# A three-stage network on one core: a first operation without data for ScalarE, other loads, and a new order of every engine's work

## The chip, the cores and the metric

The kernel runs on one core of a Trainium2 chip. Five engines work side by side: TensorE multiplies matrices (PE in the profile, and PEld for its weight loads), VectorE (DVE), ScalarE (ACT) and GpSimd (POOL) do elementwise work, and SyncE (SP) issues the DMAs that move data between HBM and the on-chip memory SBUF. TensorE writes into PSUM, which has eight banks. The metric is the device time of one execution in microseconds (us).

## The reference

Three networks stand behind each other, all in float32, for 2 batches of 768 positions.

1. Attention with 8 heads of 64 columns. A query sees the keys less than 16 positions away, and beside them 24 summaries of all keys: the maximum of each block of 32 keys, with the mean of the 32 values:

```python
k_sum = k.reshape(B, H, nb, block, D).max(axis=3)
v_sum = v.reshape(B, H, nb, block, D).mean(axis=3)
mask_l = np.abs(pos[:, None] - pos[None, :]) < window      # window = 16, block = 32
scores_l = np.where(mask_l, scale * q @ k.T, -1e9)
scores_s = scale * q @ k_sum.T + np.log(block)
a = softmax(concat([scores_l, scores_s]))
x = a @ concat([v, v_sum])
```

2. Four causal attention experts (`wq, wk, wv, wo`, 64 columns each) over the result, of which a gate (`w_gate`) mixes the best two for each position.
3. A channel mix: `k = max(xk @ w_k, 0)`, `out = sigmoid(xr @ w_r) * ((k * k) @ w_v)`, where `xk` and `xr` blend each position with the one before it.

## The kernel before

**Tiles.** Stage 1 works through 12 tiles of 128 queries, six to a batch. For each: scores (`stage1_scores`; the mask is added and the row's maximum taken by VectorE at L606, which leaves the maximum in `nm`), the exponential on ScalarE (L609, 8 a tile), the sum and its reciprocal (`rss`, L612 and L614), the normalizing product (L620 on GpSimd or VectorE, L625 on ScalarE), transposes on TensorE (`turn`, L637), and the product with the values (L679). The values' block means are matmuls too (L500), which need the values of a whole batch. Stage 2 has projections (L772 for values and gates, L754 for queries and keys), scores (L854), transposes (L637), weighted values (L952) and the output projection (L994). Stage 3 has L1146 (`rec`), L1197 (`hid`) and L1284 (`duo`); its two large products use seven block products in place of eight.

**Precision.** Operands of stages 2 and 3 are split into a high and a low half (`rnd`, L368 to L371, and `sub`, L376 to L378), and each product is three matmuls: high by high, high by low, low by high.

**Shapes of TensorE's array.** Stages 2 and 3 mostly use the whole array (128 by 128). The scores of both attentions, the transposes and the products with values use parts of it at once: 64 by 64 (L583, L588, L589), 64 rows by 128 (L637, L854), 128 rows by 64 columns (L679, L952), 128 rows by 24 (L500). Below these are called shapes, and work that follows other work of the same shape is one run.

**Loads.** All are issued by SP in one queue (`load`, L359), with at most eight at a time in flight: the ninth waits for the first. First come the queries of tile 0 and the keys of batch 0, one load for each of the four head pairs (`key_sums`), into one tile `ks` with zeros at both ends (the halo); VectorE takes their block maxima (`ksm`, L486). A slab is a tile's own piece of the keys, copied from `ks` for batch 0 and loaded for batch 1 (`slab`). The value tiles `v` (`load_v`) hold 96 rows of values and 24 rows of means, the latter written by some engine once the means are there (`put_val_sums`).

**The order.** Nothing is reordered at run time. Each step is recorded as an operation, and the table `ORDER` gives the sequence in which they are issued, four numbers to an operation, of which the remainder picks the engine where several can do it (`any_of`). `HOMES` gives each tile its buffer. An engine works through its part of the sequence strictly in turn and waits where an operand is not ready.

Of the kernel before, what the change touches and what calls it, by code (L numbers as in the profile page):

```python
# [10 lines left out]
AF = mybir.ActivationFunctionType  # L11
# [303 lines left out]
def attn_moe_rwkv(  # L315
    ctx: ExitStack,
    tc: tile.TileContext,
    qT: bass.AP,
    kS: bass.AP,
    vp: bass.AP,  # L320
    wqk: bass.AP,
    wvg: bass.AP,
# [1165 lines left out]
```

## Time and profile before

| | us |
|---|---|
| three runs | 334.40, 332.78, 333.82 (median 333.82) |
| the profiled execution | 332.78 |
| its span, first to last instruction | 331.0 |
| TensorE busy | 319.1 |
| VectorE busy | 311.3 |
| ScalarE busy | 266.8 |
| GpSimd busy | 114.0 |

The profiled execution is the fastest of the three and lies 1.04 us below their median; 1.8 us of it lie outside the span. TensorE's granted clock is 1.0 in every stretch. Busy times say how much an engine did, not who waits for whom: for that the waits of TensorE and the chain of work that ended last are read.

### The profile page before, as it was taken

The numbers are of one execution on the slowest core, as the hardware profiler recorded it, in microseconds if no ns is written. First come the engines' busy times: TensorE is split into PE (matmuls) and PEld (weight loads), VectorE is DVE, ScalarE is ACT, GpSimd is POOL, SyncE is SP. The second block draws the span as 40 slices with busy tenths as digits, with TensorE's granted clock in tenths as the row PEclk, the third lists the DMA queues.
The fourth block names the chain that finished last, engine by engine and source line by source line (L and its number), as shares of the span: only waits on it lengthen the run. The fifth ranks groups of instructions, "written<-read, shape, count | busy, mean of one in ns | idle before, by whom it ended". The sixth has DMA issues, their size and how long they took to land.

```text
span 331.0 us, 8978 instructions
## 1 busy us (share of the span) xinstructions
PE 319.1 (96%) x3296; PEld 286.8 (87%) x3296; DVE 311.3 (94%) x941; ACT 266.8 (81%) x777; POOL 114.0 (34%) x127
## 2 busy tenths in 40 slices
PE   3979999999999999999999999999999999999995
PEld 2869988888789879787776899999998899999995
DVE  3789999999999899989999999999999999999996
ACT  0989999999898779779887889889799988965360
POOL 0556872768303810432310001545036000360231
PEclk9999999999999999999999999999999999999999
DMA  7996985757242000111212001100050000021033
GB/s 247 400 395 204 305 301 189 270 152 248 92 137 64 4 0 10 59 63 65 87 43 63 3 4 61 63 0 3 0 183 10 0 0 2 18 79 52 0 113 128
DMA packets 19628, 34.08 MB, mean 103 GB/s; under 512 B 2080, under 2 KB 8480, under 8 KB 19584
## 3 DMA queue, kind: packets, MB, share of 16 engines
q1 hardware_dynamic: 19584, 33.51, 30.0%
q8 instruction: 26, 0.43, 0.5%
q14 instruction: 18, 0.15, 0.1%
HBM read 30.16 MB, written 3.15 MB: 101 GB/s over the span
## 4 chain that ended last, share of the span: by engine, by line
PE 94%; DVE 2%; DMA 2%; SPq 1%; issue 0%; ACT 0%; ACTq 0%
PE ps L1284 18%; PE ps L1197 18%; PE ps L754 11%; PE ps L1146 10%; PE ps L637 6%; PE ps L952 6%; PE ps L772 6%; PE ps L854 6%; PE ps L994 5%; PE ps L679 3%; PE ps L583 3%; DMA ks<-in_kS 2%; PE ps L588 1%; PE ps L500 1%; DVE w L606 1%; SPq L359 1%
## 5 line engine op out<-in xcount | busy, mean ns | idle before, releaser
L1284 PE MATMUL ps<-w,s 128*128 128x256 f32 x336 | 48.7, 281 | 0.0
L1284 PEld LDWEIGHTS ps<-w,s 128*128 128x128 f32 x336 | 43.9, 188 | 0.1
L1197 PE MATMUL ps<-b,w 128*128 128x384 f32 x216 | 40.3, 337 | 0.0
L1197 PEld LDWEIGHTS ps<-b,w 128*128 128x128 f32 x216 | 38.0, 188 | 0.1
L368 ACT ACTIVATE t<-ps 128x192 f32<-128x192 f32 (+1 forms) x108 | 30.9, 356 | 8.6 <-PE ps L637 4.2
L754 PE MATMUL ps<-b,w 128*128 128x384 f32 x192 | 36.6, 341 | 0.0
L1146 PE MATMUL ps<-w,b 128*128 128x512 f32 x144 | 35.8, 398 | 0.0
L754 PEld LDWEIGHTS ps<-b,w 128*128 128x128 f32 x192 | 33.2, 188 | 0.9 <-issue 0.4
L1146 PEld LDWEIGHTS ps<-w,b 128*128 128x128 f32 x144 | 26.5, 188 | 5.9 <-DVE gsum L820 0.2
L609 ACT ACTIVATE w<-w,nm 128x120 f32<-128x120 f32 x72 | 28.5, 407 | 0.9 <-DVE nm L606 0.7
L368 ACT ACTIVATE b<-ps 128x384 f32<-128x384 f32 (+4 forms) x50 | 23.8, 492 | 3.9 <-PE ps L994 1.6
L368 ACT ACTIVATE s<-u 128x512 fp32r<-128x512 f32 x24 | 14.8, 628 | 9.4 <-DVE u L1059 5.5
L1123 DVE SCALAR_TENSOR_TENSOR t<-b,mu,t 128x384 f32<-128x384 f32 x32 | 21.2, 681 | 0.8 <-ACT t L387 0.7
L854 PE MATMUL ps<-ks,b 64*128 64x384 f32 (+3 forms) x192 | 21.8, 342 | 0.0
L368 ACT ACTIVATE w<-ps 120x256 f32<-120x256 f32 (+2 forms) x49 | 19.7, 445 | 1.7 <-PE ps L1146 0.8
L952 PE MATMUL ps<-t,b 128*64 128x384 f32 (+2 forms) x144 | 20.7, 422 | 0.0
L376 DVE TENSOR_TENSOR b<-t,b 128x384 fp32r<-128x384 f32 x37 | 20.1, 567 | 0.5 <-ACT b L368 0.3
L772 PE MATMUL ps<-q,b 128*128 128x260 f32 x144 | 20.3, 290 | 0.2 <-DVE b L376 0.2
L772 PEld LDWEIGHTS ps<-q,b 128*128 128x128 f32 x144 | 18.2, 188 | 1.6 <-issue 0.5
L368 ACT ACTIVATE b<-t 128x384 fp32r<-128x384 f32 x38 | 19.0, 516 | 0.5 <-PE ps L1197 0.5
L994 PE MATMUL ps<-u,w 128*128 128x384 f32 x96 | 18.9, 338 | 0.0
L387 ACT ACTIVATE t<-b,omu 128x384 f32<-128x384 f32 x28 | 16.9, 613 | 2.2 <-PE ps L952 1.6
(202 smaller groups left out, 913.4 us busy)
## 6 DMA issues: line engine op xcount, KB each, us to landing
s<-in_wk SPq DMA_DIRECT2D x8, 512.0 KB, 4.0
s<-in_wv SPq DMA_DIRECT2D x8, 512.0 KB, 4.2
w<-in_vp SPq DMA_DIRECT2D x15, 256.0 KB, 6.5
w<-in_qT SPq DMA_DIRECT2D x12, 256.0 KB, 5.6
out_y<-t SPq DMA_DIRECT2D x24, 128.0 KB, 1.8
s<-in_wr SPq DMA_DIRECT2D x4, 512.0 KB, 5.7
s<-in_kS SPq DMA_DIRECT2D x6, 320.0 KB, 4.7
ks<-in_kS SPq DMA_DIRECT2D x4, 400.0 KB, 3.9
```

Of the source, the lines that this page charges most:

```text
L368: ways = [("act", act(n, sb), lambda: nc.scalar.activation(dst(), src(), AF.Copy)), ("dve", dve2(n) if sb else dve(n), lambda: nc.vector.t ...
L376: ways = [("dve", dve(n), lambda: nc.vector.tensor_tensor(dst(), a(), b().bitcast(F32), ALU.subtract), sb)]
L609: op("act", act(NK, True) + 186, lambda i=i, z=z, pr=pr, nm=nm: nc.scalar.activation(pr()[:, i], pr()[:, i], AF.Exp, bias=nm.t[:, i:i + 1] ...
L754: mm(p.t[:, :C], a[kc].t[:, cols], x.t[:, kc, :], start=(kc == 0 and i == 0), stop=(kc == KC - 1 and i == 2))
L772: mm(p.t[:, :260], x.t[:, kc, tok], a[kc].t, start=(kc == 0 and i == 0), stop=(kc == KC - 1 and i == 2))
L854: mm(ps[e2].t[:, :z - a], q1.t[r, x, tok], ks.t[r, y, a:z], start=n == 0, stop=n == 2)
L952: mm(acc.t[64 * e2:64 * e2 + 64, tq0 * P:(tq0 + cnt) * P], vv.t[:, kb, e * D:(e + 1) * D], th[e2].t[:, i0 * P:(i0 + cnt) * P], start=first ...
L994: mm(p.t[:, :C], a[ep].t[:, m * P:(m + 1) * P], x.t[:, ep, :], start=(ep == 0 and i == 0), stop=(ep == 1 and i == 2))
L1123: op("dve", dve(C) + 60, lambda: nc.vector.scalar_tensor_tensor(tmp(), cur(), mu.t[:, i:i + 1], tmp(), ALU.mult, ALU.add), r=rd, w=[(mb, m ...
L1146: mm(p.t, a.t[:, kc, tok], w[2](), start=(kc == 0 and i == 0), stop=(kc == KC - 1 and i == 2))
L1197: mm(p.t[:, :C], a[2]()[:, o:o + P], x.t[:, u, j], start=not (j or i), stop=j == 1 and i == 2)
L1284: mm(p.t[:, :256], x.t[:, u, j * P:(j + 1) * P], v[2]()[:, col:col + 256], start=not (j or i), stop=j == FC // 2 - 1 and i == 2)
```

## The change

- ScalarE gets a first operation that needs no data: an exponential of a small constant tile, written to `omu`, which a later operation overwrites.
- The keys stand in HBM a second time: contiguous for each head pair (`kA`) and, for batch 1, for each tile with its halo (`kT`). Batch 0's key loads carry 768 columns in place of 800; GpSimd writes the halo's zeros.
- Value tiles other than the first load their 96 own rows, where before those of the first eight tiles loaded 128.
- The three masks are three loads, the third later; the identity in `cst` is 64 columns wide in place of 128.
- `ORDER` and `HOMES` are new throughout: the order of every engine, the engine of some steps and the buffers.

```diff
@@ buffers and first operations
-    cst = buf("cst", [P, P + OWN + 16 + 2 * PAIR])
+    cst = buf("cst", [P, SUB + OWN + 16 + 2 * PAIR])
...
+    op("act", 210, lambda: nc.scalar.activation(omu.t[:, 0:1], sms.t[:, 0, 0, 1:2], AF.Exp), r=[(sms, "eps")], w=[omu])
@@ def slab(t):
-            load(lambda: k.t[:, :, NB:NB + SLAB], kS[b, :, :, tt * P:tt * P + SLAB], P * HP * SLAB * 4, 290.0,
+            load(lambda: k.t[:, :, NB:NB + SLAB], kT[tt], P * HP * SLAB * 4, 340.0,
@@ def load_v(t, s2):
-        if t < TPB + 2:
+        if t < PLAIN:
             load(lambda: v.t, vp[b, a:a + P], P * 2048, w=[(v, "win"), (v, "sum")])
         else:
             a = SUB * (2 * tt + s2) + NB
-            load(lambda: v.t[WROW[s2]], vp[b, a:a + KS0], KS0 * 2048, 230.0, w=[(v, "win")])
+            load(lambda: v.t[WROW[s2]], vp[b, a:a + KS0], KS0 * 2048, 330.0, w=[(v, "win")])
@@ def turn(banks_, c, src):
-            nc.tensor.transpose(banks_[a].t[:v.shape[1], c * SUB:(c + 1) * SUB], v, cst.t[r, r])
+            nc.tensor.transpose(banks_[a].t[:v.shape[1], c * SUB:(c + 1) * SUB], v, cst.t[r, :SUB])
@@ def raw64(src, n=1):  (the number is the planner's, not the operation's)
-        op("act", act(512, True) + 60, lambda: nc.scalar.activation(ff(), high(), AF.Abs, scale=F64_SCALE),
+        op("act", 660, lambda: nc.scalar.activation(ff(), high(), AF.Abs, scale=F64_SCALE),
@@ first loads
+    op("pool", 150, lambda: (nc.gpsimd.memset(k0.t[:, :, :HALO], 0.0), nc.gpsimd.memset(k0.t[:, :, HALO + S:], 0.0)),
+       w=[(k0, "halo")])
     load_q(0)
     for i in range(HP):
-        key_sums(0, i, k0, (lambda i=i: k0.t[:, i], lambda i=i: k0.t[:, i, HALO:HALO + S]), kS[0, :, i])
+        key_sums(0, i, k0, [lambda i=i: k0.t[:, i, HALO:HALO + S]] * 2, kA[0, i])
...
-    load(lambda: msk.t[:, 1:], masks[:, 1:], P * 2 * NK * 4, 260.0, w=[(msk, 1)])
-    load(lambda: cst.t, consts, P * 1120, 300.0, w=[cst])
+    load(lambda: msk.t[:, 1], masks[:, 1], P * NK * 4, 260.0, w=[(msk, 1)])
+    load(lambda: cst.t, consts, P * 864, 300.0, w=[cst])
@@ the order, one line of each
-    12, 0, 4, 16, 36, 44, 24, 32, 56, 52, 64, 20, 60, 236, 72, 40, 92, 48, 244, 201, 68, 28, 188, 280, 100, 792,
...
+    8032, 8172, 8036, 8052, 8008, 8176, 8012, 8141, 8224, 8180, 8192, 8056, 8144, 8228, 8060, 8232, 8064, 8196,
```

Lines after the change are one or two off: L583 is L582, L606 is L605, L637 is L636, L772 is L771, L500 is L502.

Three places show how the order moves. The first is the head of SP's queue: `w` takes queries or values, `ks` keys, `msk` masks, `b_57` the weights of values and gates (`in_wvg`). Before:

```order
L359 DMA w_63<-in_qT 128x512
L359 DMA ks_69<-in_kS 128x800 x4
L359 DMA msk_74<-in_masks 128x120
L359 DMA msk_74<-in_masks 128x240
L359 DMA w_77<-in_qT 128x512
L359 DMA w_79<-in_qT 128x512
L359 DMA cst_83<-in_consts 128x280
```

The same place after the change:

```order
L360 DMA w_63<-in_qT 128x512
L360 DMA ks_67<-in_kA 128x768 x4
L360 DMA msk_78<-in_masks 128x120
L360 DMA w_80<-in_qT 128x512
L360 DMA b_57_82<-in_wvg 128x1040
L360 DMA msk_78<-in_masks 128x120
L360 DMA w_87<-in_qT 128x512
L360 DMA cst_90<-in_consts 128x216
```

The weights of values and gates, 20th among the rows before, are now fifth, behind the keys. Further down, four loads of means from the tile `w_416` into value tiles (L541) have come into this queue, at rows 25, 27, 29 and 31, writes that GpSimd and ScalarE made before; ScalarE makes none now (before five).

The second place is VectorE in the softmax of tile 0 (`b_60`, maxima in `nm`), as it passes to tile 1 (`b_72`). Before:

```order
L606 ISA b_60_87,nm_89<-ps_135,msk_74 128x120
L606 ISA nm_89 128x1
L606 ISA b_60_87,nm_88<-ps_104,msk_74 128x120
L606 ISA nm_88 128x1
L606 ISA b_72_156,nm_158<-ps_155,msk_74 128x120
```

After the change, where `q_199`, `q_204` and `q_209` are halves of the weights `b_57`, and `s_16` is a slab that takes key maxima:

```order
L605 ISA b_60_94,nm_95<-ps_116,msk_78 128x120
L605 ISA nm_95 128x1
L370 CAST q_204<-b_57_82 128x260
L377 TENSOR_TENSOR q_209<-b_57_82,q_199 128x260
L370 COPY s_16_153<-ksm_85 128x4x24
L605 ISA b_60_94,nm_95<-ps_92,msk_78 128x120
L605 ISA nm_95 128x1
L605 ISA b_72_158,nm_159<-ps_156,msk_78 128x120
```

Three operations have come between the seventh and the eighth maximum of tile 0. `q_199` is made by GpSimd.

The third place is TensorE late in stage 2, where turns (L637, then L636) of the tile `t` stand before a product with the values (L952, then L951). Before:

```order
L1146 MATMUL ps_3425<-w_1181,b_676_3065 128x512
L637 MATMUL ps_3436<-cst_83,t_3423 128x64
L637 MATMUL ps_3437<-cst_83,t_3423 128x64
...
L952 MATMUL ps_3444<-t_3375,b_403_2105 64x384
L952 MATMUL ps_3444<-t_3390,b_403_2105 64x384
```

After the change (six turns of the tile in both lists, two of them shown):

```order
L636 MATMUL ps_3431<-cst_90,u_638_3261 128x64
L636 MATMUL ps_3448<-cst_90,t_3421 128x64
L636 MATMUL ps_3449<-cst_90,t_3421 128x64
...
L951 MATMUL ps_3457<-t_3359,b_403_2135 64x384
L951 MATMUL ps_3457<-t_3380,b_403_2135 64x384
```

The turns of `t` now follow other turns, where before they followed a product on the whole array. Over the whole list the number of runs by shape is this, where the first L772 is the first matmul of stage 2:

| runs of one shape | whole array | 64 rows by 128 | 128 by 64 | 64 by 64 | 128 by 24 | sum |
|---|---|---|---|---|---|---|
| before, up to the first L772 | 0 | 3 | 2 | 4 | 3 | 12 |
| after, up to the first L771 | 0 | 4 | 2 | 3 | 4 | 13 |
| before, from there on | 23 | 33 | 16 | 6 | 2 | 80 |
| after, from there on | 18 | 27 | 16 | 6 | 2 | 69 |

The matmuls themselves are the same in number on every line, on either side of that point.

## Rows read from the trace of the kernel before

**Rows 1.** The page, busy time of each engine: us, share of the span, instructions.

```profile
PE 319.1 (96%) x3296; PEld 286.8 (87%) x3296; DVE 311.3 (94%) x941; ACT 266.8 (81%) x777; POOL 114.0 (34%) x127
```

**Rows 2.** Waits of TensorE: who waited for whom, total us, times, longest.

```profile
PE ps L588 <- DMA ks<-in_kS: 4.7, 1, 4.7
PE ps L583 <- ACT b L625: 1.7, 1, 1.7
PE ps L589 <- DVE ksm L486: 1.4, 4, 0.4
PE ps L772 <- DVE b L376: 0.2, 1, 0.2
```

**Rows 3.** Busy time by stretch: length, then PE, PEld, DVE, ACT, POOL; clock, DMA share.

```profile
0.00:26.50 26.50, 18.37 (x456) 15.28 (x456) 17.50 (x96) 16.19 (x63) 10.89 (x23) 1.00 0.95 345
26.50:60.00 33.50, 33.49 (x477) 30.45 (x481) 32.51 (x133) 31.94 (x137) 21.35 (x24) 1.00 0.75 254
270.00:327.20 57.20, 57.20 (x482) 56.92 (x481) 56.60 (x118) 35.51 (x71) 15.45 (x8) 1.00 0.15 50
327.20:331.00 3.80, 0.01 (x1) 0.00 (x0) 0.85 (x2) 0.00 (x0) 0.00 (x0) 1.00 0.30 104
```

**Rows 4.** The same view, VectorE alone, seven stretches from 26.5 to 327.2.

```profile
sum 300.70, DVE 292.95; mean DVE 41.85
```

**Rows 5.** The chain that ended last, early: start, us, what.

```profile
2.60 6.08 DMA ks<-in_kS
...
24.33 0.42 DVE q L369 x2
24.74 0.91 DVE q L376
...
26.51 1.53 PE ps L772 x9
```

**Rows 6.** The chain later, on TensorE.

```profile
76.95 0.72 PE ps L854 x6
77.68 0.18 PE ps L637 x6
...
98.66 1.58 PE ps L994 x9
100.24 2.10 PE ps L754 x12
...
104.44 2.11 PE ps L994 x12
106.55 0.33 PE ps L637 x6
106.88 2.30 PE ps L754 x12
```

**Rows 7.** Timeline of ScalarE, early: start, us, operation.

```profile
8.77 1.28 ACT L368 ACT_TABLE_LOAD   x1 [8.77 <-DMA ks<-in_kS]
...
10.88 0.38 ACT L609 ACTIVATE b<-b,nm 128x120 f32<-128x120 f32 x1
```

**Rows 8.** Timeline of VectorE: the first maximum read, and a copy at 40.7.

```profile
9.77 0.08 DVE L606 DVE_READ_ACCUMULATOR2_ANT nm<- 128x1 f32 x1
...
40.74 0.96 DVE L369 COPY s<-ksm 128x96 f32<-128x96 f32 x1
```

**Rows 9.** Timeline of GpSimd: weights rounded at 29.5, a product at 40.7.

```profile
29.51 1.06 POOL L371 TENSOR_SCALAR w<-s 128x512 fp32r<-128x512 f32 x1
...
40.65 0.99 POOL L620 TENSOR_TENSOR w<-w,rss 128x480 f32<-128x480 f32 x1
```

**Rows 10.** The page, DMA issues: KB each, median us from issue to landing.

```profile
s<-in_wqk SPq DMA_DIRECT2D x2, 512.0 KB, 6.6
```

**Rows 11.** Groups by line and shape: the low half of an operand, GpSimd and VectorE.

```profile
L378 POOL TENSOR_TENSOR s<-u,s 128x512 fp32r<-128x512 f32 x1 | 3.0, 3046 | 5.3 <-ACT s L368 5.3
L376 DVE TENSOR_TENSOR s<-u,s 128x512 fp32r<-128x512 f32 x23 | 16.2, 711 | 0.0
```

More of the change, by code (lines that the diff above doesn't have):

```diff
@@ L318, in attn_moe_rwkv @@
     qT: bass.AP,
-    kS: bass.AP,
+    kA: bass.AP,
+    kT: bass.AP,
     vp: bass.AP,
@@ L466, in slab @@
             rnd("dve", lambda: k.t[:, :, NB:NB + SLAB], lambda: k0.t[:, :, tt * P:tt * P + SLAB], HP * SLAB,
-                [(k0, i) for i in range(HP)], [(k, "win")], True)
+                [k0], [(k, "win")], True)
     def load_v(t, s2):
@@ L484, in key_sums @@
             ksm[b] = buf("ksm", [P, HP, NB])
-        load(tf[0], src, P * (S if b else SPV) * 4, w=[(tb, i)])
+        load(tf[0], src, P * S * 4, w=[(tb, i)])
         op("dve", dve(S), lambda: nc.vector.tensor_reduce(
@@ L521, in sums1 @@
             t = buf("s4", [P, S])
-            key_sums(1, i, t, [lambda t=t: t.t] * 2, kS[1, :, i, HALO:HALO + S])
+            key_sums(1, i, t, [lambda t=t: t.t] * 2, kA[1, i])
         p = [bank("ps")] * 2
@@ L540, in put_val_sums @@
             ], r=[vsm[b]], w=[(v, "sum")], issue=850)
-    def ident():
-        return cst.t[:, 0:P]
     def own(j, s2=None):
-        o = P + OWN - NB - 4 * j
+        o = SUB + OWN - NB - 4 * j
         if s2 is not None:
-            o = P + OWN + 16 + s2 * PAIR + NB - 2 - (4 * j + 2 * s2)
+            o = SUB + OWN + 16 + s2 * PAIR + NB - 2 - (4 * j + 2 * s2)
         return cst.t[:, o:o + NB]
@@ L570, in stage1_scores @@
             ps = [bank("ps") for par in range(2)]
-            kr = [(x, i) for x in (k0, ksm[0]) for i in range(lo, hi)] if t < EARLY else [k]
+            kr = [(x, i) for x in (k0, ksm[0]) for i in range(lo, hi)] + [(k0, "halo")] if t < EARLY else [k]
             for i in range(lo, hi):
@@ L607, in stage1_softmax @@
                     pr()[:, i], p.t[:, i * NK:(i + 1) * NK], msk.t[:, m], -0.125, BIG, ALU.add, ALU.min,
-                    nm.t[:, i:i + 1]), r=[(p, i), (msk, min(m, 1))], w=[key[i], (nm, i)])
+                    nm.t[:, i:i + 1]), r=[(p, i), (msk, m)], w=[key[i], (nm, i)])
                 op("act", act(NK, True) + 186, lambda i=i, z=z, pr=pr, nm=nm: nc.scalar.activation(
@@ L798, in lt @@
         def lt():
-            return cst.t[:, P + OWN:P + OWN + 16].rearrange("p (o a c) -> p o a c", o=1, a=E).to_broadcast(sh)
+            return cst.t[:, SUB + OWN:SUB + OWN + 16].rearrange("p (o a c) -> p o a c", o=1, a=E).to_broadcast(sh)
         def wide(v):
@@ L1346, in attn_moe_rwkv @@
     load_q(3)
+    load(lambda: msk.t[:, 2], masks[:, 2], P * NK * 4, 260.0, w=[(msk, 2)])
     load(lambda: mu.t, mus, 4096, w=[mu])
@@ L1414, in attn_moe_rwkv @@
     plan.run(alloc)
-_ORDER = ["qT", "kS", "vp", "wqk", "wvg", "wo", "wk", "wv", "wr", "mus", "masks", "tri", "consts"]
+_ORDER = ["qT", "kA", "kT", "vp", "wqk", "wvg", "wo", "wk", "wv", "wr", "mus", "masks", "tri", "consts"]
 def _layout(
@@ L1427, in _layout @@
     ks[..., HALO:HALO + S] = k.reshape(B, HP, 2, S, D).transpose(0, 2, 4, 1, 3)
-    d["kS"] = ks.reshape(B, P, HP, SPV)
+    d["kA"] = k.reshape(B, HP, 2, S, D).transpose(0, 1, 2, 4, 3).reshape(B, HP, P, S)
+    ks = ks[1].reshape(P, HP, SPV)
+    d["kT"] = np.stack([ks[:, :, t * P:t * P + SLAB] for t in range(TPB)])
     vp = np.zeros((B, VROWS, DM), f)
@@ L1466, in _layout @@
     lt = np.broadcast_to((np.arange(E)[None, :] < np.arange(E)[:, None]).astype(f).reshape(1, 16), (P, 16))
-    d["consts"] = np.concatenate([np.eye(P, dtype=f), own, lt, pair.reshape(P, 2 * PAIR)], axis=1)
+    d["consts"] = np.concatenate([np.tile(np.eye(SUB, dtype=f), (2, 1)), own, lt, pair.reshape(P, 2 * PAIR)], axis=1)
     return d
```

276 rows, old and new, of tables (HOMES, ORDER) are left out of this document.

## The prediction

> **What bounds the kernel now.** I read the busy times first: TensorE works 319.1 of 331.0 us and VectorE 311.3 [rows 1], so either could be the bound. The waits decide: TensorE waits 4.7 us for the first keys, 1.4 for key maxima, 1.7 at a score, 0.2 at its first projection, and at nothing else worth a row [rows 2]. By stretch, it is idle 8.1 us before 26.5 us (26.50 less 18.37), hardly at all from there to 327.2, and 3.8 us at the end, when the last result is added, multiplied and stored [rows 3]. VectorE is nearly as full: 292.95 of those 300.7 us [rows 4]. The kernel thus has three parts: a start up to the first projection at 26.51 us [rows 5], 300.7 us in which matmuls stand end to end, and a tail. With equal matmuls, time can come from an earlier start, from what TensorE loses between matmuls, and from the tail.
>
> One such loss shows in the chain. Twelve matmuls of L754 take 2.10 us behind L994, which uses the whole array too, and 2.30 behind turns: 0.20 for going back to the whole array. Six turns take 0.18 us behind L854, of the same shape, and 0.33 behind L994: 0.15 for entering a divided shape [rows 6]. A busy TensorE hides these, since the profile counts them as work.
>
> **The change part by part.**
>
> *Fewer changes of shape.* From the first projection on there are 80 runs of one shape before and 69 after. Runs on the whole array fall from 23 to 18: 5 times 0.20 is 1.0 us. The others fall from 57 to 51: 6 times 0.15 is 0.9. Together 1.9 us, in the stretch where TensorE is never idle, so the whole of it counts, if its operands come as much sooner. VectorE must follow: by the changed counts in the two orders, each times its group's mean duration, its 311.3 us fall by about 3.8 (the largest piece is three `s<-u,s` fewer at 0.71, 2.1 us [rows 11]; additional copies take some of it back), while ScalarE gains about 1.1 us and GpSimd about 3.6, with 64 and 217 us idle [rows 1]. So VectorE doesn't become the bound by its sum. With 11 runs at 0.15 to 0.20 each, the term lies between 1.65 and 2.2.
>
> *ScalarE's first operation.* The table load, 1.28 us, began at 8.77 when the last keys had landed, then a slab copy, and the first exponential stood at 10.88 [rows 7], though its maximum was read by 9.85 (9.77 and 0.08) [rows 8]. With the load in idle time before the keys, the exponentials can start some 0.9 us sooner; the slab copy stays ahead of them. At worst nothing, if another engine is last.
>
> *Keys and their halo.* The four key loads are 1,536 KB in place of 1,600. The last landed 6.08 us after its issue began [rows 5], with the others in front: 64 of 1,600 of that is 0.24 us; I take 0.2. Contiguity I cost at nothing; no row has such a load alone. GpSimd writes the zeros in its first two microseconds, while the keys are on their way. `kT` and the smaller constants come where no DMA is waited for [rows 2]; the third mask is needed only by tile 5. Nothing for these.
>
> *Value rows.* Fourteen loads lose 64 KB each, 0.9 MB. In the first 26.5 us the DMA engines are 95% busy, at 345 GB/s [rows 3], so the four or five of them that lie there save at most about 0.9 us of transfers. TensorE waits there for no values: 0, at best 0.9.
>
> *Weights of values and gates.* Moved from 20th to fifth in SP's queue, behind the keys and the second queries, 520 KB earlier than some masks, queries, constants and values. These have time: TensorE takes up the first values only after the scores of three tiles. In return VectorE's casts and low halves of these weights, 0.42 and 0.91 us on the chain at 24.33 [rows 5], come away from the spot just ahead of the first projection: up to 1.3 us. But two of them, and a copy of key maxima, now stand ahead of the eighth maximum of tile 0, and ScalarE's exponential of it, with all of tile 1's behind, waits for that.
>
> What this costs hangs on GpSimd. The trace has such a copy at 40.74: it took 0.96 us for 96 elements a partition, and ended as a GpSimd product begun at 40.65 ended, 0.99 later [rows 8, 9]. It was held up. In the new place GpSimd is rounding the same weights. If each of the three is held up for most of a GpSimd operation, some 0.5 us each, ScalarE loses about 1.5 us; if none, nothing. The Trainium skill, in SBUF — State Buffer, section "Who interferes with whom", says that a VectorE copy or cast in its faster mode, or an operation on two SBUF inputs beside a GpSimd read, shares a port pair with GpSimd that is held for the whole instruction, so that the later one waits. The trace agrees at 40.74.
>
> *Means through SP.* Four small loads now wait in SP's queue for the means. Behind them stand the second half of the weights of queries and keys, batch 1's keys, the triangle mask, the output weights. In the old kernel GpSimd took up that half at 29.51 [rows 9]. Such loads take 6.6 us to land [rows 10], so one issued by 22.9 is in time. I expect the means near 20; cost 0, and up to 2 us if they came 2 us after 22.9. ScalarE is rid of five writes, before the first projection and soon after.
>
> *Start, summed.* 0.2 for the keys, up to 0.9 for ScalarE, up to 1.3 for the weights: 2.4 at best; 0 when the copies are held up. I take the middle, 1.2. One more run of a shape in the start costs 0.15 at most and is in that. The tail has the same steps in the same order: 0.
>
> *Sum.* 1.9 and 1.2 make 3.1 us. The profiled execution, 332.78, becomes 329.7; it lies 1.04 below the median of 333.82, so a median of **330.7 us** is my forecast. Its own range is 329.0 to 332.0.
>
> **The rivals.**
>
> *The three copies are held up.* If GpSimd blocks each, as at 40.74 [rows 8, 9], the 1.5 us on ScalarE's chain outweigh its 0.9 and most of the weights' gain; the start comes out even and only the runs pay: 332.78 less 1.9 and plus 1.04, 331.9. For it speaks the one case that the trace has; against it, that the weights may land when GpSimd is between two operations. This is what the rule of SBUF — State Buffer would make of the new place.
>
> *The time comes back as waits.* The early gain goes as above, and inside the long stretch VectorE, at 97% [rows 4], is late now and then by a tenth or two, since a new order over so many steps has new tight spots; ten or so of those eat the 1.9. For it: VectorE's share, and that a search aims at planned times, not real ones. Against it: the old order was such a plan too, and TensorE waits 0.2 us in its long stretch. The time would be 333 to 334, say 333.5.
>
> *Slower: low halves on GpSimd in the last stage.* Four operands of L1284 get their low half `s<-u,s` from GpSimd, where before it was one, and two others of a like kind. GpSimd takes 3.05 us for it, VectorE 0.71 [rows 11]. Where the product stands less than 3 us behind its high half, TensorE waits up to 2.3 us each, 9.4 in all, in a stretch with no slack. That gives 330.7 and 9.4, 340.1 at most. It decides against the change once more than 4.8 us of it show: three of the four uncovered. Against it: the one before was covered, and GpSimd idles for most of that stretch, 15.45 of 57.2 us busy [rows 3].
>
> *Everything early pays.* The start gains 2.4, the runs 2.2 and the lighter DMA load 0.5: 5.1 off, 328.7.
>
> **How the numbers follow.** Chances: forecast 0.50, copies held up 0.20, waits 0.16, slower 0.08, everything early 0.06. About 0.5% (1.7 us) is what a measurement of this kernel can tell from no change. Faster by more than that is below 332.15: nearly all of the forecast's share, over half of the first rival's and the last case, 0.66. Within 0.5% is the rest of these and the waits, 0.25. Slower is 0.09: the GpSimd case and a little of the waits. For 8 times in 10 the range reaches from the last case, 328.7, to the second rival's 333.6.
>
> **What would show it.** In the new profile the table load should end before 4 us and the first exponential start near 10.0. The first L771 should start near 25.3 (26.51 less 1.2), with L605 of tile 0's eighth maximum after 12 us if the copies are held up. From there to the last matmul should be 298.8 us (300.7 less 1.9), still with no wait over 0.5 us. VectorE should be busy near 307. Wrong would be: a first L771 later than 26.5, or new waits of TensorE on VectorE or GpSimd behind it that add to 2 us or more. The L1283 stretch should still run end to end, with no `s<-u,s` of GpSimd as what ended a wait.

## The result, and the profile after

The forecast was 330.7 us. Measured was 338.85 us (median of 5 runs, 338.39 to 339.4) against 334.4 for the kernel before (5 runs, 332.78 to 334.8): ratio 1.0144, 95% interval 1.0115 to 1.0173. The change makes the kernel slower, and the forecast was wrong. The profiled execution has a span of 337.1 us, 6.1 longer than that of before.

The page first, busy time of each engine, in answer to [rows 1]:

```profile
PE 320.0 (95%) x3296; PEld 288.3 (86%) x3296; DVE 319.3 (95%) x933; ACT 269.0 (80%) x778; POOL 124.6 (37%) x136
```

VectorE has 8 operations fewer and works 8.0 us longer. At the kernel before's mean durations the new counts would have given 3 to 4 us less; so the same operations have become about 11 us longer in all. GpSimd's have grown by 5.9 us in the same way. Next, who TensorE waited for (as [rows 2]: total us, times, longest):

```profile
PE ps L587 <- DMA ks<-in_kA: 4.8, 1, 4.8
PE ps L582 <- issue: 1.4, 1, 1.4
PE ps L588 <- DVE ksm L488: 1.3, 4, 0.4
PE ps L678 <- DMA w<-in_vp: 1.2, 1, 1.2
PE ps L636 <- DVE b L619: 1.1, 1, 1.1
PE ps L853 <- DVE ks L377: 0.8, 1, 0.8
PE ps L853 <- DVE b L377: 0.7, 2, 0.6
PE ps L636 <- DVE b L370: 0.7, 1, 0.7
PE ps L753 <- DVE b L377: 0.6, 1, 0.6
PE ps L1283 <- DVE b L1169: 0.3, 1, 0.3
```

The first three and the L636 behind L619 lie before the first projection. The other waits, 4.3 us, lie in the stretch in which TensorE of before never waited. They cost more than is shown, since a matmul's end is modelled: from the start of one matmul to the start of the next, eight gaps behind the first projection are 0.40 to 1.39 us wider than is usual for their form, 6.0 us in sum, and in the old trace none there is wider by 0.4. They end at 32.2, 46.4, 49.9, 74.3, 122.6, 140.4, 159.5 and 278.3 us.

By stretch, as [rows 3] and, for VectorE alone over six stretches, [rows 4]:

```profile
0.00:26.50 26.50, 17.87 (x440) 14.94 (x442) 18.38 (x90) 16.35 (x70) 12.64 (x28) 1.00 0.93 300
```

```profile
sum 306.03, DVE 298.96; mean DVE 49.83
```

The long stretch takes 306.0 us in place of 300.7. In the start the DMA engines are as busy as before (0.93 and 0.95) and move 300 GB/s in place of 345. The same kernel run again (below) has 306.5 us in the long stretch, and its first projection at 25.85 us, where this execution has it at 27.07 and the kernel before at 26.51: the long stretch repeats, the start doesn't. TensorE's granted clock is 1.00 over the long stretch both times.

What holds VectorE up is seen at 119 us. Timeline: start, us, operation, and in brackets the idle time before and who ended it.

```profile
119.46 1.28 POOL L379 TENSOR_TENSOR w<-s,w 128x512 fp32r<-128x512 f32 x1 [0.48 <-ACT w L369]
...
119.52 1.50 DVE L1058 TENSOR_TENSOR s<-s 128x256 f32<-128x256 f32 x1
...
120.95 0.68 DVE L377 TENSOR_TENSOR s<-s,s 128x512 fp32r<-128x512 f32 x1
121.55 0.41 DVE L1058 TENSOR_TENSOR s<-s,s 128x256 f32<-128x256 f32 x1
121.89 0.68 DVE L377 TENSOR_TENSOR b<-ps,b 128x512 fp32r<-128x512 f32 x1
...
122.62 0.38 PE L853 MATMUL ps<-ks,b 64*128 64x256 f32 x1 [0.58 <-DVE b L377]
```

A VectorE operation that takes 0.42 us when free begins 0.06 us behind a GpSimd operation, takes 1.50 and ends 0.28 us after GpSimd is done at 120.74. Behind it stands the subtraction out of PSUM (`b<-ps,b`) that TensorE needs; its operands were ready at 118.9. The same picture stands ahead of the waits at 32.2, 140.4, 159.5 and 278.3 us: a VectorE operation 0.8 to 1.1 us too long, begun while GpSimd runs a TENSOR_TENSOR, and ended 0.3 to 0.6 us behind it. At 49.9 it is less direct: VectorE is held for 1.1 us at 45.57, and TensorE waits for a ScalarE copy that stands behind an exponential begun at 48.13, just behind VectorE's maximum. That this is one chain is read from the times; no wait names it. Against the shortest fifth of its form (operation and shape, forms with ten operations or more), 15 VectorE operations are over 0.6 us too long, 14.1 us together; in the old trace there are 4, 3.3 us together, none ahead of a wait. None of these reads or writes PSUM.

### The profile page after: what moved, and what is told of

Its sections match the earlier page's. It is cut to its first block, busy times and chain, and to the rows that moved or that the text cites. A ratio compares the mean times of both kernels' runs of the same rounds, so it can differ in the third digit from the quotient of the medians.

```text
span 337.1 us, 8990 instructions
## 1 busy us (share of the span) xinstructions
PE 320.0 (95%) x3296; PEld 288.3 (86%) x3296; DVE 319.3 (95%) x933; ACT 269.0 (80%) x778; POOL 124.6 (37%) x136
## 5 line engine op out<-in xcount | busy, mean ns | idle before, releaser
L1196 PE MATMUL ps<-b,w 128*128 128x384 f32 x216 | 40.3, 337 | 0.0
L753 PE MATMUL ps<-b,w 128*128 128x384 f32 x192 | 37.5, 340 | 0.6 <-DVE b L377 0.6
L369 ACT ACTIVATE t<-ps 128x192 f32<-128x192 f32 (+1 forms) x101 | 28.2, 343 | 6.2 <-PE ps L636 3.3
L1145 PEld LDWEIGHTS ps<-w,b 128*128 128x128 f32 x144 | 26.5, 188 | 5.9 <-DVE nm L860 0.2
L369 ACT ACTIVATE b<-ps 128x384 f32<-128x384 f32 (+4 forms) x54 | 25.6, 485 | 5.2 <-PE ps L1196 2.4
L379 POOL TENSOR_TENSOR w<-s,w 128x512 fp32r<-128x512 f32 x14 | 22.8, 1633 | 7.6 <-ACT w L369 7.1
L369 ACT ACTIVATE b<-t 128x384 fp32r<-128x384 f32 x42 | 20.8, 519 | 0.8 <-PE ps L1196 0.6
L951 PE MATMUL ps<-t,b 128*64 128x384 f32 (+2 forms) x144 | 20.7, 423 | 0.0
L771 PE MATMUL ps<-q,b 128*128 128x260 f32 x144 | 20.2, 288 | 0.0
L369 ACT ACTIVATE w<-ps 120x256 f32<-120x256 f32 (+2 forms) x44 | 16.6, 423 | 3.3 <-PE ps L1145 1.2
L377 DVE TENSOR_TENSOR b<-t,b 128x384 fp32r<-128x384 f32 x35 | 19.2, 562 | 0.0
L388 ACT ACTIVATE t<-b,omu 128x384 f32<-128x384 f32 x31 | 18.3, 612 | 1.1 <-DVE u L377 1.0
L853 PEld LDWEIGHTS ps<-ks,b 64*128 64x128 f32 x192 | 15.7, 186 | 4.0 <-DVE b L377 1.1
```

What stands on the lines that cost most here:

```text
L369: ways = [("act", act(n, sb), lambda: nc.scalar.activation(dst(), src(), AF.Copy)), ("dve", dve2(n) if sb else dve(n), lambda: nc.vector.t ...
L377: ways = [("dve", dve(n), lambda: nc.vector.tensor_tensor(dst(), a(), b().bitcast(F32), ALU.subtract), sb)]
L379: ways.append(("pool", pool_tt(n), lambda: nc.gpsimd.tensor_tensor(dst(), a(), b().bitcast(F32), ALU.subtract)))
L753: mm(p.t[:, :C], a[kc].t[:, cols], x.t[:, kc, :], start=(kc == 0 and i == 0), stop=(kc == KC - 1 and i == 2))
L771: mm(p.t[:, :260], x.t[:, kc, tok], a[kc].t, start=(kc == 0 and i == 0), stop=(kc == KC - 1 and i == 2))
L853: mm(ps[e2].t[:, :z - a], q1.t[r, x, tok], ks.t[r, y, a:z], start=n == 0, stop=n == 2)
```

## The experiments

All times are against the kernel before on the same chip (its medians 333.3 to 334.0). Op lines are one to six off in these kernels.

**The edits in the old order.** `ORDER` and `HOMES` of before, the new first operation, loads and constants.

> The changed code (first ScalarE operation, new key and value loads, smaller constants) with the order and the buffers of the kernel before. Theory A, the new order is what costs: near the kernel before, 332.5 to 334.5 us (338.9 for the changed kernel), no wait of TensorE over 0.5 us behind its first projection. Rival B, the edits to the loads cost: 337 us or more, with DMA waits in the first 50 us.

Measured: 335.81 us, ratio 1.0067 (1.0041 to 1.0093). Neither theory: the edits alone cost 0.7%, and in the trace nearly all of it before the first projection, which starts at 30.06 us; behind that there is one wait. From the first projection to the last matmul the profiles in the old order, with any of the edits below, take 300.7 to 301.5 us; the changed kernel's two take 306.0 and 306.5. So what the edits cost lies in the start, and what the new order costs lies behind it. For the start, the DMA engines tell a first part. Between 16 and 24 us (packets, MB, mean rate), before, and with the edits in the old order:

```profile
DMA packets 1342, 3.24 MB, mean 405 GB/s; under 512 B 148, under 2 KB 148, under 8 KB 1340
```

```profile
DMA packets 972, 2.04 MB, mean 255 GB/s; under 512 B 241, under 2 KB 241, under 8 KB 970
```

Both have the engines busy all the time; a packet of 2048 bytes took 86 ns on average, and 134 with the edits. The changed kernel has 262 GB/s there, and 120 ns.

The second part is TensorE's clock. In this profile TensorE stood 2.67 us until 23.85, and from 22.7 to 29.5 us its clock was granted at 0.50, the lower of its two levels (1.2 in place of 2.4 GHz). Thirty score matmuls then took 1.87 us; the next experiment, with the clock granted in full, has 1.04 for the same thirty. The stretch, these matmuls, and those of the next experiment:

```profile
22.70:29.50 6.80, 5.65 (x95) 5.11 (x97) 3.25 (x13) 2.24 (x6) 2.73 (x4) 0.50 1.03 296
```

```profile
23.85 1.87 PE L577 MATMUL ps<-s,w 64*64 64x120 f32 x30 [2.67 <-issue]
```

```profile
21.36 1.04 PE L577 MATMUL ps<-s,w 64*64 64x120 f32 x30 [1.47 <-ACT b L619]
```

From the end of the stop to the first projection it is 6.2 us here and 4.0 there, so 2.2 us of the late projection are the clock's. The profiled execution, 336.79, is 1 us above the median; two others, with a mean granted clock of 0.998 and 0.999, took 335.9 and 335.7, so the loss in the median isn't the clock's alone.

**The old order with 128 rows.** One edit undone:

```diff
-        if t < PLAIN:
+        if t < TPB + 2:
             load(lambda: v.t, vp[b, a:a + P], P * 2048, w=[(v, "win"), (v, "sum")])
```

> As the first experiment (changed code, order and buffers of before), but value loads of the first eight tiles carry 128 rows again. Theory D, loads of 96 rows slow the DMA engines (2048 byte packets took 129 to 141 ns between 16 and 24 us, 85 to 88 with 128 rows): packets back at 84 to 90 ns, the 2.9 us wait near 21 us back at 1.9 or less, 332 to 333.5 us, so 2 to 3 us below the first experiment. Rival, another edit (keys by head pair, the third mask load) slows them: 335 to 336 us as in the first.

Measured: 333.02 us, ratio 0.998 (0.9958 to 1.0001), and between 16 and 24 us

```profile
DMA packets 1392, 3.18 MB, mean 398 GB/s; under 512 B 268, under 2 KB 268, under 8 KB 1390
```

So theory D holds in this order: with value loads that lost a quarter of their rows the packets beside them are slow too (those of 4096 bytes took 274 ns, 167 here), and that costs 0.9%. Small packets aren't the reason: there are more under 512 bytes here than with 96 rows. The first projection is at 25.34 us. TensorE's waits in the whole trace; the last is the first projection's own, and only the L577 behind `w` (at 59.2 us) lies behind it:

```profile
PE ps L582 <- DMA ks<-in_kA: 4.6, 1, 4.6
PE ps L577 <- ACT b L619: 1.5, 1, 1.5
PE ps L583 <- DVE ksm L483: 1.3, 4, 0.4
PE ps L577 <- ACT w L364: 0.6, 1, 0.6
PE ps L766 <- DVE b L372: 0.2, 1, 0.2
```

**96 rows in every second load**, against the old order with the edits:

```diff
-        if t < PLAIN:
+        if t < PLAIN or t < TPB + 2 and s2 == 0:
```

> Order of before, changed code; of each pair of value tiles the first is loaded with 128 rows, the second with 96 into partitions 0 to 95 (in the change the first goes to 24 to 119). If the place from 24 is what slows the DMA engines: 2048 byte packets at 84 to 92 ns between 16 and 24 us and 333 us, as with 128 rows. If the count of 96 does it: 100 to 130 ns, 334 to 335.5 us.

Measured: 335.38 us, 1.0039 (1.0017 to 1.006); packets of 2048 bytes at 109 ns on average, and

```profile
DMA packets 1141, 2.56 MB, mean 319 GB/s; under 512 B 212, under 2 KB 212, under 8 KB 1139
```

Half the short loads are gone, and under half of the rate and of the loss come back. These short loads begin at partition 0, so the place from 24 on isn't needed for the slowing. What in a load of 96 rows slows the engines, no run shows.

**VectorE's order: seven steps.** Each `b<-ps,b` or its like goes ahead of the SBUF steps that were held. At 119 us, for one (rows of VectorE's order):

```diff
+L377 TENSOR_TENSOR b<-ps,b
 L1058 TENSOR_TENSOR s<-s
 L377 TENSOR_TENSOR s<-s,s
 L1058 TENSOR_TENSOR s<-s,s
-L377 TENSOR_TENSOR b<-ps,b
```

> The changed kernel, with seven VectorE steps that read PSUM and that TensorE waits for put ahead of the SBUF-to-SBUF steps that stood before them; no work changes. Theory A, one VectorE step is held until a GpSimd step ends, and only steps with both ends in SBUF are held: the waits at 32.2, 49.9, 122.6, 140.4, 159.5, 278.3 and 298.5 us (0.7, 0.4, 0.7, 0.9, 1.0, 0.45 and 0.3) go or shrink, 338.9 - 4 = about 335 us. Rival C, VectorE has too much work there and anything late is waited for: the waits come back at the next step, 338 to 339.5 us.

Measured: 340.87 us, 1.0225 (1.0179 to 1.027): slower still. The gaps at 122, 140 and 159 us fell from 2.6 us to 0.85, but one of the moved steps was itself waited for (`s<-b,s`, 1.5 us at 303), and TensorE waited 1.3 us for a VectorE step at 259 us, where the changed kernel had no wait. The one profiled execution was 4.1 us above the median; TensorE also stood 3.2 us until 48.6 for GpSimd, which took up the output weights 1.7 us later than in the changed kernel's trace, and from 47.5 to 54.3 us its clock was granted at 0.50. So its gaps don't divide the median.

**Four of these steps alone**, those at 122, 140, 159 and 278 us, moved in the same way.

> The changed kernel with its loads as they are, and four VectorE steps that read PSUM ahead of SBUF-to-SBUF steps that GpSimd holds up (those ahead of the waits at 122, 140, 159 and 278 us: 0.7, 0.9, 1.0 and 0.45 us). Theory A: 2 to 2.5 us less than the changed kernel (338.1 on this chip's last call), about 335.8 us, ratio to before near 1.006. Rival C, VectorE is full there and the waits come back elsewhere: 337.5 to 338.5 us, ratio 1.010 to 1.014.

Measured: 336.52 us, 1.0098 (1.0066 to 1.0129); the changed kernel run again beside the later kernels,

> The changed kernel itself, on the chip of the three that follow, as their base: 338 to 340 us, with a 2048 byte packet at 110 to 140 ns between 16 and 24 us (84 to 88 in the kernel before).

had 338.07, 1.0122 (1.0089 to 1.0154), so the same as in its first runs. The four gaps fell as expected, from 3.0 us to 0.85 in the trace; 1.5 came back at 252 us. In the median the moves are worth 0.2 to 0.5%, within the intervals, so the 2 to 2.5 us of theory A didn't come. At 252 us the same GpSimd operation went two ways. In the changed kernel:

```profile
250.06 1.02 DVE L377 TENSOR_TENSOR b<-t,b 128x384 fp32r<-128x384 f32 x2
250.54 4.79 POOL L379 TENSOR_TENSOR w<-s,w 128x512 fp32r<-128x512 f32 x1 [3.02 <-ACT w L369]
251.00 0.69 DVE L1044 SCALAR_TENSOR_TENSOR s<-s 128x512 int32<-128x512 int32 x1
251.60 1.02 DVE L1058 TENSOR_TENSOR b<-b,b 128x384 f32<-128x384 f32 x2
...
254.08 1.49 DVE L1169 TENSOR_TENSOR b<-ps,b 128x384 f32<-128x384 f32 x3
```

With the four moves:

```profile
246.03 1.02 DVE L372 TENSOR_TENSOR b<-t,b 128x384 fp32r<-128x384 f32 x2
246.51 1.70 POOL L374 TENSOR_TENSOR w<-s,w 128x512 fp32r<-128x512 f32 x1 [3.03 <-ACT w L364]
246.97 1.78 DVE L1039 SCALAR_TENSOR_TENSOR s<-s 128x512 int32<-128x512 int32 x1
...
248.68 1.84 DVE L1053 TENSOR_TENSOR b<-b,b 128x384 f32<-128x384 f32 x2
...
252.57 0.44 PE L1191 MATMUL ps<-b,w 128*128 128x384 f32 x1 [1.31 <-DVE b L1164]
```

In the first trace VectorE keeps the way, and GpSimd stands until VectorE turns to operands in PSUM at 254.08. In the second GpSimd gets in at once, VectorE's next two rows take 1.1 and 0.8 us more, and TensorE waits. Both began at the same point of VectorE's work. Of nine profiles in the new order with GpSimd's steps unchanged, four show the first way and five the second; what decides, no run shows.

**GpSimd's steps off the path.** Of GpSimd's steps beside which VectorE was held, eight are left out, and later eleven (seven of these and four others): ScalarE copies the first operand in place of the difference.

```diff
+            off = len(plan.ops) in OFF
-            ways.append(("pool", pool_tt(n), lambda: nc.gpsimd.tensor_tensor(
-                dst(), a(), b().bitcast(F32), ALU.subtract)))
+            ways.append(("pool", pool_tt(n), lambda: nc.scalar.activation(dst(), a(), AF.Copy) if off else
+                         nc.gpsimd.tensor_tensor(dst(), a(), b().bitcast(F32), ALU.subtract)))
```

> The changed kernel, with eight of GpSimd's subtractions left out: ScalarE copies the minuend into the low half in their place (0.63 us each). They are the eight that ran while a VectorE step ahead of a TensorE wait was long. Theory A: those VectorE steps fall from 1.5-1.8 us to 0.4-0.9, the seven waits go, about 334.5 us. Rival C: VectorE has the same work, 338 to 339.5 us.

> The changed kernel in its own order, with eleven of GpSimd's steps (nine subtractions, two differences) left out and ScalarE copying the first operand in their place: all beside which, in any profile of the new order so far, a VectorE step that TensorE then waited for took 0.5 us or more too long. Theory A: no such wait is left (4 to 5 us in the changed kernel behind its first projection): ratio to before 0.998 to 1.004, 333 to 335 us. Rival, VectorE is late for its own amount of work: ratio 1.010 or more, 337 us and over.

Measured: with eight 337.99 us, 1.0119 (1.0086 to 1.0152), no better than the changed kernel run again; its one profile, 3.9 us above the median, also has the wait at 257 us (1.3 us). With eleven 335.89 us, 1.0062 (1.0039 to 1.0084). TensorE's waits behind the first projection with eleven:

```profile
PE ps L580 <- DVE nm L858: 0.5, 1, 0.5
PE ps L634 <- DVE b L367: 0.4, 1, 0.4
PE ps L634 <- ACT t L366: 0.4, 1, 0.4
PE ps L676 <- DMA w<-in_vp: 0.2, 1, 0.2
PE ps L851 <- DVE b L374: 0.2, 1, 0.2
```

From 140 us to the end no wait of 0.2 us is left, and VectorE, with the same 933 operations, is busy 315.3 us in place of 319.3: there it was late because it was held, not because it had too much to do. Against the changed kernel's two ratios that is 0.6 to 0.8%, 2 to 2.7 us, clear of both intervals, but less than theory A gave. The long stretch takes 302.8 us. Between 43 and 49 us four gaps are wider than usual by 1.8 us in sum, more than this kernel's whole lag behind that of before at the end of the trace (1.4); the first of them is behind a load. GpSimd's steps that were kept hold VectorE there; one of them:

```profile
43.43 1.60 POOL L378 TENSOR_TENSOR w<-s,w 128x512 fp32r<-128x512 f32 x1
...
43.81 1.54 DVE L1034 TENSOR_SCALAR s<-s 128x512 f32<-128x512 f32 x1
```

Behind it stands the maximum that TensorE's wait of 0.5 us at 45.88 is for (`nm L858`, above). What these holds have in the 1.8 us was not measured by itself.

**The value loads of tile 3 earlier in SP's queue**, ahead of most of batch 1's keys and of the last write of means (rows of SP's order):

```diff
 DMA s<-in_kA 128x768
 DMA u<-w 24x512
+DMA w<-in_vp 96x512
+DMA w<-in_vp 96x512
 DMA s<-in_kA 128x768
 DMA p<-w 24x512
```

> The changed kernel, with the two value loads of tile 3 ahead of the third summary load of batch 1's keys in SP's queue, issued near 25 us in place of 36.5 and 37.7. If the 1.2 us wait for values at 46.4 us is the queue's doing and nothing takes its place: 337.5 us. Rival, DMA bandwidth: the tiles land early but another load lands as much later, 338.5 to 339 us.

Measured: 339.47 us, 1.0195 (1.015 to 1.0239). The wait for values is gone from the trace, and the total is no better: TensorE waits 0.6 us at 46 for VectorE instead, and the wait at 255 us is there (1.3 us).

**128 rows in the new order.** First for eight tiles, the edit as in the old order, with five writes of means moved behind the loads that they follow on:

> The changed kernel with value loads of 128 rows for the first eight tiles; five writes of means into these tiles move behind their loads in the order. Theory D: packets at 84 to 90 ns, the wait for values at 46 us gone, 2 to 3 us less than the changed kernel: 336 to 337 us; what is left above the kernel before is the new order's. If the order's head rather than the rows makes the loads late: no change, 338.5 to 339.5 us.

It says nothing on the rows: 350.66 us, ratio 1.0485, since a write of means that waits for its load stops all that is queued behind it (TensorE waits 5.9 us at 45 for a GpSimd step, and twice more for over 2 us). The clock was granted at 0.50 three times, from 41.3, 58.3 and 89.1 us on, 13.6 us in sum, so the price is that of the waits and of the slower matmuls together. With the four moves on VectorE on top,

> The kernel just before, with four VectorE steps that read PSUM ahead of SBUF-to-SBUF steps that GpSimd holds up (those ahead of the waits at 122.6, 140.4, 159.5 and 278.3 us). Theory A: these waits, 0.7, 0.9, 1.0 and 0.45 us, shrink to under 0.3 each and nothing takes their place: 2 to 2.5 us less than without it, about 334.3 us. Rival C, VectorE is full there: within 0.7 us of the kernel without it.

it had 347.38, 1.0406, so these gave 3.3 us there, with the clock at 0.50 for as long. Then for tiles 1 and 2 alone, with no step moved:

```diff
-        if t < PLAIN:
+        if t < EARLY:
```

> The changed kernel, order untouched, but the four value loads of tiles 1 and 2 carry 128 rows again (those of tiles 3 to 7 keep 96, since their means are written earlier). Theory D: 2048 byte packets at 84 to 92 ns between 16 and 24 us (105 to 111), first projection 0.5 to 1 us earlier, waits before 50 us shorter: 336 to 337 us, ratio 1.006 to 1.010. Rival, in the new order nothing waits for those loads: 338 us, ratio 1.012.

Measured: 339.72 us, 1.0197 (1.0166 to 1.0228). Packets of 2048 bytes took 88 ns again, the first projection came at 26.01 us, and it wasn't faster: the gain that theory D promised doesn't come in this order. Between 20 and 28 us SP's queue issues so little that 1.38 MB move (2.85 before), and the wait for values at 45 us is 1.9 us. Then the four moves on VectorE on top, and a fifth, for the gap at 254 us, of the same form (`b<-ps,b` ahead of the steps that GpSimd holds):

> The kernel just before with five VectorE steps that read PSUM moved ahead of SBUF-to-SBUF steps: the four of the ninth experiment, and the one that TensorE waited for 1.5 us at 252 us there. Theory A: 2 to 3.5 us less than without the moves, 333.5 to 334.5 us, ratio 1.000 or a little under. Rival C: within 1 us of the kernel without them.

Measured: 338.49, 1.0152 (1.0116 to 1.0188), 1.2 us less, within the two intervals. A gap of 0.8 us at 254 stayed; against the kernel without the moves, new ones stood at 33.6 (1.6 us, for a VectorE maximum) and, 0.4 and 0.7, at 283 and 287 us.

**ScalarE's first operation alone**, in the kernel before:

```diff
+    op("act", 210, lambda: nc.scalar.activation(omu.t[:, 0:1], sms.t[:, 0, 0, 1:2], AF.Exp), r=[(sms, "eps")], w=[omu])
```

> The kernel before with ScalarE's first operation without data alone. The prediction's term: first exponential at 10.0 us in place of 10.88, up to 0.9 us of the start gone, 332.8 to 333.5 us (before 333.7 on this chip), the first projection at 25.6 to 26.4 us in place of 26.5. Rival, loads set the start whatever ScalarE does: no change, first projection at 26.5 us.

Measured: 333.35 us, 0.9985 (0.9963 to 1.0007). The first exponential is at 9.69 us in place of 10.88, the first projection at 26.39 in place of 26.51: next to nothing of the gain arrives.

**A version meant to beat both.** The old order with 128 rows, and a tile's keys earlier in SP's queue:

```diff
 DMA s<-in_vp 128x2x512
+DMA s<-in_kT 128x4x160
 DMA s<-in_vp 128x2x512
 DMA s<-in_wr 128x1024
-DMA s<-in_kT 128x4x160
```

> Order of before, changed code, 128 rows of values for the first eight tiles, and in SP's queue tile 6's keys ahead of the third load of batch 1's values, behind which they waited until 51.7 us and came 0.6 us late for the scores at 59.2 us. If the late keys cost what TensorE waits: 0.6 us below the kernel without the move (333.0, ratio 0.998), ratio 0.996. Rival, the values or another load is late by as much: ratio 0.998.

Measured: 333.4 us, 0.9984 (0.9961 to 1.0007). The wait at 59 us is gone, the gain isn't there; its first projection lay at 26.93 us. With or without the move this version beats the changed kernel by 1.4% (333.0 to 333.4 against 338.1), but can't be told from the kernel before.

## Why the prediction was wrong

**The step that failed** is "VectorE doesn't become the bound by its sum", and with it "still with no wait over 0.5 us". Its sum took mean durations of the old trace as if they belonged to the operations. They belong to the operations beside that order of GpSimd's: VectorE was to be busy near 307 us and was 319.3. Nor is the sum what matters: five times an operation was held 0.8 to 1.1 us just ahead of one that TensorE needed, 3.8 us of the 6.0 in the eight gaps, and at 49.9 (0.4 us) by way of ScalarE. Of the rest, 1.4 us at 46.4 is behind a load. Taking away eleven GpSimd steps took away the waits from 140 us on (shown); moving single VectorE steps took some away and brought others. Both signs that the prediction named as wrong came: a first projection later than 26.5, and more than 2 us of new waits on VectorE. The second came again when the kernel was run again, the first didn't.

The prediction had both halves of this. It read one held copy in the old trace [rows 8, 9] and applied it to the three copies at the start alone. And the rival of waits that come back was right in kind: it reckoned with ten waits of a tenth or two, 333.5 us, where there were eight of 0.4 to 1.4. The Trainium skill's rule in SBUF — State Buffer, section "Who interferes with whom", that the port pair is held for a whole instruction and the later one waits, fits the held operations. At 250 us GpSimd was kept out over seven instructions.

**Fewer changes of shape:** right, a little smaller. 80 runs became 69, and the widened gaps at a change (those under 0.3 us) sum to 10.8 us before and 9.1 to 9.3 after, by how the change at 122.6 us is counted: about 1.5 us, where 1.9 was forecast.

**ScalarE's first operation:** the table load ended at 2.02 us and the first exponential stood at 10.17:

```profile
0.74 1.28 ACT L424 ACT_TABLE_LOAD   x1 [0.74 <-PEq L1481]
...
10.17 0.40 ACT L608 ACTIVATE b<-b,nm 128x120 f32<-128x120 f32 x1
...
13.32 0.39 ACT L608 ACTIVATE b<-b,nm 128x120 f32<-128x120 f32 x1 [0.39 <-DVE nm L605]
```

That answers [rows 7]: 0.7 us won. But nearly none of it reaches the first projection, by the run that has this edit alone. And 0.39 go at the eighth exponential to the three operations ahead of its maximum, which began at 13.01 us, past the 12 that was the sign: the held-up rival at a quarter of its price. Of the three the copy was held, as at 40.74: it took 0.74 us and ended 0.05 behind a GpSimd subtraction.

The start's term, 1.2 us, was wrong in the profiled execution: the first L771 came at 27.07 us, 0.6 later than before. When the same kernel was run again it came at 25.85, 0.7 sooner, so one execution doesn't size this term. In the other kernels it lay between 25.3 and 27.0 us but for three (27.6 to 30.9). In these three, and in no other profile, TensorE's granted clock fell to 0.50 ahead of it, behind a stop of TensorE of 2.0 to 3.1 us near 21. This stop varies from none to 3.1 us; ScalarE's product ends it in most kernels of the old order, and in the new order the profile mostly names nothing. What sets it stays open.

**Value rows:** forecast 0, at best 0.9 us gained. Bytes were counted, the rate was taken as given. In the old order these rows cost 2.9 us (shown), by slower loads and, in the profiles, a longer stop with a lower clock behind it. In the new order the rate is as low, but putting back the four loads where no step had to move brought nothing.

**Means through SP:** cost 0 was wrong as far as the wait goes, 1.2 us. The weights' second half was issued at 22.1 us, in time as reckoned; but SP then stood from 26.9 to 31.6 us, tile 3's values were issued at 36.5 and 37.7, and TensorE waited 1.2 us for them at 46.4. With these loads earlier the wait went and the time didn't, so what it costs in the total isn't shown.

**Slower by low halves on GpSimd:** there are four of them. Their mean of 2.4 us, against 3.0 for the one before [rows 11], hides two kinds: three took 1.5 to 1.6 us, and one, at 307.7, took 4.9 beside VectorE's work in SBUF:

```profile
L379 POOL TENSOR_TENSOR s<-u,s 128x512 fp32r<-128x512 f32 x4 | 9.6, 2402 | 22.5 <-ACT s L369 13.1 <-issue 9.3
```

No matmul waited for one. What two of them did was hold VectorE, at 276 and 294 us, for 0.45 and 0.3 us of gaps.

**The sum.** TensorE's long stretch is 5.3 us longer: 6.0 in eight gaps, about 1.5 less for the shapes, and 0.8 spread over smaller gaps. With the start's 0.6 that is 5.9 us in the profiled execution, where 3.1 the other way were forecast. How the 4.5 us between the medians divide over the causes is shown only in part: the steps held by the eleven GpSimd operations 2 to 2.7; rows and queues can't be added up, since one hides the other. The 2.1 us that the kernel without the eleven still lies above the kernel before stay open.

## What to carry to other kernels

A duration in a trace holds for the neighbours that the operation had: where VectorE and GpSimd both work in SBUF, look for operations much longer than the shortest of their form, and in a new order ask what stands behind each that meets a GpSimd operation. What showed in the time here was taking such GpSimd operations away; putting single steps out of PSUM ahead of the SBUF steps that are held took gaps away, and others came. Count a transfer by its rate as well as its bytes: here fewer rows moved more slowly. Before a late start is explained by waits alone, read TensorE's granted clock in it: it was at half in three of these kernels' starts.

## What was not expected of the hardware

- Loads of 96 rows of 2048 bytes, in place of 128, in the old order, brought packets of 2048 bytes from 86 to 134 ns on average and those of 4096 from 162 to 274 (405 to 255 GB/s, engines busy all the time); with every second load at 96 rows it was 319 GB/s.
- A GpSimd subtraction of 128 by 512 takes 1.28 us free and took 4.79 us beside a run of VectorE operations in SBUF; the same one took 1.70 in another run, and VectorE paid.
- A stop of TensorE can cost more than its length: during one of 2.67 us the granted clock fell to 0.50 and stayed there until 5.7 us behind its end, and matmuls that take 4.0 us up to the first projection took 6.2.
